# Attention feeding a feed-forward layer on one core: the order of two middle periods, and where one transpose, one copy and some stores stand

## The chip, the core and the metric

The kernel runs on one core of a Trainium2 chip. The metric is the device time of one execution in microseconds (us); the median of 3 runs of the kernel before is 207.83 us (207.78 to 207.98). The profiled execution has a span of 205.9 us, and its granted TensorE clock was 1.00 throughout. Engine names are those of the profile: PE multiplies matrices (PEld is its loading of weights), DVE is the vector engine, ACT the scalar engine, POOL issues the loads, SP issues stores and DMA transposes.

## What is computed

Attention with a local band of 96 keys and 8 global keys, over 4 batches, 8 heads, 768 rows and 64 elements per head. Its output, 3072 rows of 512, goes through a feed-forward layer with a squared ReLU.

```python
# q, k, v: (4, 8, 768, 64);  w_in: (512, 2048);  w_out: (2048, 512)
scores = q @ k.T / sqrt(64) + bias(head, distance)     # -1e9 outside band and globals
a = softmax(scores)
x = (a @ v) with heads side by side                    # (3072, 512)
h = x @ w_in
g = s * maximum(h, 0)**2 + b
out = g @ w_out                                        # (3072, 512), float32
```

## The kernel before

The rows are cut into 12 granules of 256 rows, three to a batch. Granules 0, 3, 6 and 9 are the first of their batch and need no older keys; the others do, through the copies `ko` and `vo`. A period j overlaps three granules: the attention of granule j, the first product (`P1`) of granule j-1 and the second product of granule j-2. For granules 0 to 2 the second product is plain (`P2`); from 3 on (`W0 = 3`) it is a Strassen-like scheme of seven products (`W_mm`) with sums made on DVE (`W_tw` of weights, `W_sw` of values). The order of instructions on every engine is the order of the calls in the program, and each engine works through its own list in order.

The helpers that matter, with the lines of the kernel before under which the profile files their instructions:

```python
def S_mm(j, hp):    # L414 PE: scores of one pair of heads into PSUM "scA" or "scB"
def S_post(j, hp):  # L427 ACT: exp;  then S_mul, L437/L441 DVE: times the template
def A(j, hp, tag):  # L470 PE: values times scores;  A_norm, L487+L488 DVE: divide
                    #   (tags "av": 1 buffer, "psh": 2 buffers, shared with P1)
def KO(j):          # L338+L341 DVE: keys of older blocks for granule j
def XB(j):          # L319, L327 SP: DMA transposes of keys and queries
def XT_dma(j):      # L531 SP: DMA transpose of x
def P1(j, fp, sq):  # L552 PE: 8 matmuls of 256 columns;  L568/L570 ACT: ReLU;
                    #   square: "act" on ACT at once (L576); "late" on DVE where Q()
                    #   is called (L589); else on DVE at the next PE group (L543)
def P2_mm(j, tb, part):   # L622 PE: 4 matmuls of 512 columns per part
def P2_raw(j, tb):        # L655 ACT: s * product, without the row vector bvec
def P2_bias(j, tb):       # L660 DVE: + bvec, and a store
def W_mm(j, n):           # L735 PE: 8 matmuls of 256 columns

def VO(j):                # values of older blocks
    ...
    nc.vector.tensor_copy(vo[:, :, :, 0:65], vaug[...])               # L363
    nc.vector.tensor_copy(vo[0:NG, :, :, 0:65], vaug[...broadcast])   # L366

def XT_pe(j, eng="act", tag="pso"):
    ... 8 x nc.tensor.transpose(...)        # L500 PE
    nc.scalar.copy(xT[j][:], ps[:])         # L506 ACT

def wsum_fin():
    ps = ps_h.tile([P, DM], F32, name="ps_b", tag="psh")
    ... 2 matmuls                                              # L613 PE
    nc.vector.tensor_scalar_mul(bvec[:], ps[:], b_bc[:])       # L614 DVE

def P2_out(j, tb):        # L640 DVE: s * product + bvec
    ...
    if tb == 1:
        P2_store_all(j)   # one store of 512 KB on SP
```

Periods 3 and 4 are built by `period`, which takes products from a list between the parts of the attention:

```python
def period(j, items, at, late=None, mid=()):
    SS(j, (0, 1))              # scores, exp, template of two pairs of heads
    run(items, at[0])
    A(j, 0)
    run(items, at[1])
    A(j, 1, "psh")
    run(list(mid), 100)
    SS(j, (2, 3))
    if j == 3:
        pace(pts[j, 2][0:1, 0, 0:1])
        load_granule(6)
    run(items, at[2])
    A(j, 2)
    if at[3]:
        KO(j + 1)
    run(items, at[3])
    A(j, 3, "psh")
    ...
    if late is None:
        XT_dma(j)
    if j + 1 < NJ:
        VO(j + 1)
    if j + 2 < NJ:
        XB(j + 2)
    if late is not None:       # period 3: wsum_fin, then x of granule 3
        run(items, 1)
        late()
        XT_pe(j, "act", "psh")
    run(items, 100)

P2b(0); P2b(1)                 # P2 of granule 1, second half, parts 0 and 1
for f in range(4):
    P1(2, f, "act" if f % 2 else "late")
Q(2, 0); Q(2, 2)
period(3, [P2b 2, P2b 3, P1(2, 4..7), P2(2, 0..3), P2_bias(0, 0), P2_bias(0, 1),
           P2_store_all(0)], (3, 1, 3, 1), wsum_fin, (W_tw 3 in two halves))

# [...] period 4: at = (4, 2, 3, 0), mid = (W_tw 2 second half, P2_bias(1, 1))
items = [(P1, 3, 0, "act"), (P2, 2, 4), (P1, 3, 1), (W_tw, 2, 0, 4)]
items += [(P2, 2, 5), (P2_bias, 1, 0)]
items += [(P1, 3, 2, "late"), (P1, 3, 3, "late"), (P2, 2, 6), (Q, 3, 2), (Q, 3, 3)]
items += [(P1, 3, 4, "act"), (P2, 2, 7), (P1, 3, 5, "act"), (P1, 3, 6),
          (W_tw, 4, 0, 4), (P1, 3, 7), (W_sw, 3, 3), (flush,), (W_tw, 4, 4, 8)]
```

From period 5 on `steady(j)` is used, which the change leaves as it is. It begins: scores of pairs 0 and 1, `W_mm(j-2, 1)`, `W_mm(j-2, 2)` (into "scA", so after the exp of the first scores), `P1` of j-1 twice, `A(j, 0)`, `P1`, `A(j, 1)`; on DVE the template products, `W_post` and `W_sw` stand between them.

Of the kernel before, what the change touches and what calls it, by code (L numbers as in the profile page):

```python
# [18 lines left out]
def kernel(  # L19
# [62 lines left out]
    def bg(j):  # L82
        return divmod(j, NGR)
# [33 lines left out]
    def load_granule(j):  # L117
        load_rows(j, "k")
        load_rows(j, "q")
        load_v(j)  # L120
# [3 lines left out]
    def pace(t):  # L124
        nc.gpsimd.tensor_copy(pdum[:], t)  # L125
# [183 lines left out]
    def XB(j, nms="kq"):  # L309
        if "k" in nms:  # L310
            XBk(j)
        if "q" in nms:
            XBq(j)
# [18 lines left out]
    def KO(j):  # L332
        b, g = bg(j)
        if g == 0:
            return
        ko = work.tile([P, HP, GB, P], BF16, name="ko", tag="ko", bufs=2)
        lo = (g * GB - 1) * P
        nc.vector.tensor_copy(  # L338
            ko[:].rearrange("p h a c -> p h (a c)"), kT[b % 2][:, :, lo : lo + GT]
        )  # L340
        nc.vector.tensor_copy(  # L341
            ko[:, :, :, 0:NG],
            kT[b % 2][:, :, 0:NG].unsqueeze(2).to_broadcast((P, HP, GB, NG)),
        )
        kos[j] = ko
# [9 lines left out]
            ko[:, :, :, 0:NG], kT[0][:, :, 0:NG].unsqueeze(2).to_broadcast((P, HP, GB, NG))  # L355
        )

    def VO(j):
        b, g = bg(j)
        if g == 0:  # L360
            return
        vo = work.tile([P, GB, H, VW], BF16, name="vo", tag="vo", bufs=2)
        nc.vector.tensor_copy(  # L363
            vo[:, :, :, 0:65], vaug[b % 2][:, g * GB - 1 : (g + 1) * GB - 1, :, 0:65]
        )
        nc.vector.tensor_copy(  # L366
            vo[0:NG, :, :, 0:65],
            vaug[b % 2][0:NG, 0:1, :, 0:65].to_broadcast((NG, GB, H, 65)),
        )
        vos[j] = vo  # L370

    sps = {}

# [69 lines left out]
    def SS(j, hps, which=None):  # L443
        for hp in hps:
            S_mm(j, hp, which=which)
        for hp in hps:
            S_post(j, hp)

    def A(j, hp, tag="av", norm=True, av=None):
        b, g = bg(j)  # L450
        first = g == 0
        pt = pts.pop((j, hp))
        if j not in xn:
            xn[j] = xpool.tile([P, GB, H, D], BF16, name="xn", tag="xn", bufs=2)
        if av is None:
            av = PS[tag].tile([P, GB, 2, 65], F32, name="ps_av", tag=tag)
        for i in range(GB):
            for hi in range(2):
                h = 2 * hp + hi
                if first:  # L460
                    ops = [(i, vaug[b % 2][:, i, h, 0:65])]
                    if i == 1:
                        ops.append((2, vaug[b % 2][:, 0, h, 0:65]))
                else:
                    ops = [
                        ((0, 2)[i], vaug[b % 2][:, g * GB + i, h, 0:65]),
                        ((1, 3)[i], vos[j][:, i, h, 0:65]),
                    ]
                for n_, (c, vv) in enumerate(ops):
                    nc.tensor.matmul(  # L470
                        av[:, i, hi, :],
                        lhsT=pt[:, hi, c * P : (c + 1) * P],
                        rhs=vv,
                        start=n_ == 0,
                        stop=n_ == len(ops) - 1,
                    )
        avs[j, hp] = av
        if norm:
            A_norm(j, hp)
            flush()  # L480
# [12 lines left out]
        )  # L493

    def XT_pe(j, eng="act", tag="pso"):
        xT[j] = xpool.tile([P, KC, GT], BF16, name="xT", tag="xT")
        ps = PS[tag].tile([P, KC, GT], BF16, name="ps_x", tag=tag)
        for hp in range(HP):
            for i in range(GB):
                nc.tensor.transpose(  # L500
                    ps[:, hp, i * P : (i + 1) * P],
                    xn[j][:, i, 2 * hp : 2 * hp + 2, :],
                    ident[:],
                )
        if eng == "act":
            nc.scalar.copy(xT[j][:], ps[:])  # L506
        else:
            nc.vector.tensor_copy(xT[j][:], ps[:])

    def XT_half(j, half, eng, tag):  # L510
        if half == 0:
# [16 lines left out]
    def XT_dma(j):  # L528
        xT[j] = xpool.tile([P, KC, GT], BF16, name="xT", tag="xT")
        for i in range(GB):  # L530
            nc.sync.dma_start_transpose(  # L531
                xT[j][:, :, i * P : (i + 1) * P],
                xn[j][:, i, :, :].rearrange("p h d -> p (h d)"),
            )
# [52 lines left out]
    def Q(j, fp):  # L587
        gs = late_sq.pop((j, fp))
        nc.vector.tensor_tensor(gs, gs, gs, ALU.mult)  # L589
# [18 lines left out]
        nc.vector.tensor_tensor(hl[:, 1, :], wsum[:, 0, :], hl[:, 0, :], ALU.subtract)  # L608

    def wsum_fin():  # L610
        ps = ps_h.tile([P, DM], F32, name="ps_b", tag="psh")
        for i in range(2):
            nc.tensor.matmul(ps[:], lhsT=ones_f[:], rhs=hl[:, i, :], start=i == 0, stop=i == 1)  # L613
        nc.vector.tensor_scalar_mul(bvec[:], ps[:], b_bc[:])  # L614
# [22 lines left out]
    def P2_out(j, tb):  # L637
        b, g = bg(j)
        o_sb = o_tile(j, tb)
        nc.vector.scalar_tensor_tensor(  # L640
            out=o_sb,
            in0=po[j, tb],
            scalar=s_bc[:],
            in1=bvec[:],
            op0=ALU.mult,
            op1=ALU.add,
        )
        if tb == 1:
            P2_store_all(j)

    raw = {}

    def P2_raw(j, tb):
        o_sb = o_tile(j, tb)
        nc.scalar.activation(o_sb, po[j, tb], ACT.Copy, scale=s_bc[:])  # L655
        raw[j, tb] = o_sb

    def P2_bias(j, tb, store=True):
        o_sb = raw[j, tb]
        nc.vector.tensor_tensor(o_sb, o_sb, bvec[:], ALU.add)  # L660
        if store:
            P2_store(j, tb)

    def P2_store_all(j):
        b, g = bg(j)
        t0 = b * S + g * GT
        nc.sync.dma_start(
            out[t0 : t0 + GT, :].rearrange("(i p) c -> p i c", p=P), o_t[j][:]
        )

    def P2_store(j, tb):
        b, g = bg(j)
# [101 lines left out]
    def W_rows(j):  # L774
        b, g = bg(j)
        t0 = b * S + g * GT
        return out[t0 : t0 + GT, :].rearrange("(p r) c -> p r c", r=2)

    def W_store(j):
        nc.sync.dma_start(W_rows(j), wt[j, "o"][:])  # L780

    def W(j, n, *sums):
        W_mm(j, n)
# [198 lines left out]
    def run(items, n):  # L982
        for _ in range(n):
            if items:
                f, *a = items.pop(0)
                f(*a)

    def P2b(c):
        if c == 0:
            po[1, 1] = ps_o.tile([P, DM], F32, name="ps_2", tag="pso")[:]  # L990
        P2_mm(1, 1, c)
        if c == 3:
            P2_raw(1, 1)

    def period(j, items, at, late=None, mid=()):
        SS(j, (0, 1))
        run(items, at[0])
        A(j, 0)
        run(items, at[1])
        A(j, 1, "psh")  # L1000
        run(list(mid), 100)
        SS(j, (2, 3))
        if j == 3:
            pace(pts[j, 2][0:1, 0, 0:1])
            load_granule(6)
        run(items, at[2])
        A(j, 2)
        if at[3]:
            KO(j + 1)
        run(items, at[3])  # L1010
        A(j, 3, "psh")
        if not at[3]:
            KO(j + 1)
        if late is None:
            XT_dma(j)
        if j + 1 < NJ:
            VO(j + 1)
        if j + 2 < NJ:
            XB(j + 2)
        if late is not None:  # L1020
            run(items, 1)
            late()
            XT_pe(j, "act", "psh")
        run(items, 100)

    P2b(0)
    P2b(1)
    for f in range(4):
        P1(2, f, "act" if f % 2 else "late")
    Q(2, 0)  # L1030
    Q(2, 2)
    period(
        3,
        [
            (P2b, 2),
            (P2b, 3),
            (P1, 2, 4),
            (P1, 2, 5, "act"),
            (P1, 2, 6, "act"),
            (P1, 2, 7, "act"),  # L1040
            (P2, 2, 0),
            (P2, 2, 1),
            (P2, 2, 2),
            (P2, 2, 3),
            (P2_bias, 0, 0, False),
            (P2_bias, 0, 1, False),
            (P2_store_all, 0),
        ],
        (3, 1, 3, 1),
        wsum_fin,  # L1050
        ((W_tw, 3, 0, 4), (W_tw, 3, 4, 8)),
    )

    def P1s(j, fp, n):
        P1(j, fp)
# [82 lines left out]
        r(7)  # L1138
        W_sw(m, 3)

    for j in range(4, NJ):
        m, l = j - 1, j - 2
        if l < W0:
            items = [(P1, m, 0, "act"), (P2, l, 4), (P1, m, 1), (W_tw, 2, 0, 4)]
            items += [(P2, l, 5), (P2_bias, 1, 0)]
            items += [(P1, m, 2, "late"), (P1, m, 3, "late"), (P2, l, 6), (Q, m, 2), (Q, m, 3)]
            items += [(P1, m, 4, "act"), (P2, l, 7), (P1, m, 5, "act"), (P1, m, 6), (W_tw, 4, 0, 4), (P1, m, 7), (W_sw, m, 3), (flush,), (W_tw, 4, 4, 8)]
            period(j, items, (4, 2, 3, 0), mid=((W_tw, 2, 4, 8), (P2_bias, 1, 1, False)))
        else:
            steady(j)  # L1150
    l, m = NJ - 2, NJ - 1
    r = lambda f: P1(m, f, "late")
    Q(l, 7)
# [72 lines left out]
```

The softmax here doesn't subtract the row's maximum and nothing guards it: scores larger than these inputs give would overflow.

## Time and profile before

| | busy us | share of the 205.9 us span |
|---|---|---|
| PE | 198.5 | 96% |
| PEld | 160.6 | 78% |
| DVE | 173.4 | 84% |
| ACT | 115.9 | 56% |
| POOL | 73.2 | 36% |

In the trace period 3 begins with the score matmuls at 50.92 us, period 4 at 62.42 us, and period 5, the first steady one, at 76.04 us. In those two periods DVE is busy 10.49 of 11.50 us and 12.98 of 13.62 us. Matmuls overlap in the pipeline: the time that one takes in a group's mean is longer than the step from its start to the start of the next one, so PE's pace is read from a run of equal matmuls, and a wait from a step that is longer than that.

### The profile page before, as it was taken

Reading aid. Unit: us, or ns where it says so; the run is one execution under the profiler, and the core shown is the slowest. Engines: PE = TensorE matmul, PEld = TensorE weight load, DVE = VectorE, ACT = ScalarE, POOL = GpSimd, SP = SyncE. Lnnn points to the kernel's source line nnn. Section 1 sums busy time; section 2 is a strip of 40 time slices with the busy share of each in tenths; the row PEclk is TensorE's granted clock in tenths of the full one; section 3 lists DMA queues with packets and bytes.
Section 4 is the critical chain, followed back from the end, with each engine's and each line's share of the span. In section 5 each row is a group of like instructions: output and inputs, shape, how many; then the busy total and the mean of one; then the engine's idle time right before and its main releaser. Section 6 shows DMA issues by size and latency. Waiting matters only on the chain.

```text
span 205.9 us, 5597 instructions
## 1 busy us (share of the span) xinstructions
PE 198.5 (96%) x2286; PEld 160.6 (78%) x2293; DVE 173.4 (84%) x415; ACT 115.9 (56%) x174; POOL 73.2 (36%) x98
## 2 busy tenths in 40 slices
PE   7988999999999999999999999999999999999993
PEld 2667776547766678988988988988988988988883
DVE  5897677699989989788799799788799799787693
ACT  5887588355878576536536536536446446424400
POOL 8993683848274019009009119019000000000000
PEclk9999999999999999999999999999999999999999
DMA  5999999999999969969999969999975140040022
GB/s 164 193 184 197 192 194 193 181 154 145 148 133 150 237 83 99 194 137 118 108 227 109 208 91 106 204 109 121 204 85 140 42 133 23 0 153 5 0 105 102
DMA packets 103962, 27.64 MB, mean 134 GB/s; under 512 B 91392, under 2 KB 102016, under 8 KB 103936
## 3 DMA queue, kind: packets, MB, share of 16 engines
q0 software_dynamic: 70976, 13.11, 83.5%
q1 hardware_dynamic: 31904, 13.64, 33.8%
q10 hardware_dynamic: 1056, 0.52, 0.9%
q8 instruction: 18, 0.29, 0.6%
q14 instruction: 8, 0.07, 0.2%
HBM read 27.26 MB, written 6.29 MB: 163 GB/s over the span
## 4 chain that ended last, share of the span: by engine, by line
PE 81%; DMA 5%; POOL 5%; DVE 4%; ACT 2%; issue 1%; SPq 0%; POOLq 0%; ACTq 0%
PE ps L552 37%; PE ps_w L735 15%; PE ps_wb L735 7%; PE ps L622 6%; PE ps_av L470 4%; PE ps_wa L735 4%; DMA w_in_bf<-in_moe_w_in_dram 4%; PE ps_s L414 4%; POOL vaug L112 2%; PE ps_2s L622 2%; DVE pt L441 2%; DMA xT<-xn 1%; DVE o_pr L660 1%; POOL w_in_bf L129 1%; ACT pt L427 1%
## 5 line engine op out<-in xcount | busy, mean ns | idle before, releaser
L552 PE MATMUL ps<-xT,w_in_bf 128*128 128x256 bf16 x768 | 96.5, 273 | 2.1 <-DMA w_in_bf<-in_moe_w_in_dram 1.2
L552 PEld LDWEIGHTS <-w_in_bf 128*128 128x128 bf16 x768 | 72.6, 98 | 13.0 <-DMA w_in_bf<-in_moe_w_in_dram 2.3
L570 ACT ACTIVATE gT<-ps 128x512 bf16<-128x512 f32 x72 | 43.1, 598 | 58.5 <-PE ps L552 56.4
L427 ACT ACTIVATE pt<-ps_s 128x1024 bf16<-128x1024 f32 (+1 forms) x48 | 43.0, 950 | 4.0 <-PE ps_s L414 4.0
L735 PEld LDWEIGHTS <-sw 128*128 128x128 bf16 x288 | 28.1, 98 | 3.4
L589 DVE TENSOR_TENSOR gT<-gT 128x512 bf16<-128x512 bf16 x73 | 27.6, 415 | 1.7 <-ACT gT L570 1.6
L112 POOL DMA_DIRECT2D vaug<-in_v_dram x24 | 21.6, 912 | 4.1 <-DMA w_out_bf<-in_moe_w_out_dram 1.7
L441 DVE TENSOR_TENSOR pt<-pt,tmpl 128x1024 bf16<-128x1024 bf16 x31 | 20.7, 686 | 2.1 <-ACT pt L427 2.1
L735 PEld LDWEIGHTS <-gT 128*128 128x128 bf16 x208 | 19.8, 98 | 3.2 <-issue 0.2
L488 DVE TENSOR_TENSOR xn<-ps_av,rc 128x256 bf16<-128x256 f32 x48 | 20.4, 424 | 1.7
L125 POOL COPY pdum<-xT 1x1 bf16<-1x1 bf16 x5 | 2.5, 509 | 50.5 <-DMA xT<-xn 50.5
L622 PE MATMUL ps<-w_out_bf,gT 128*128 128x512 bf16 x74 | 18.8, 379 | 0.4 <-issue 0.2
L735 PE MATMUL ps_w<-tw,sw 128*128 128x256 bf16 x144 | 18.7, 273 | 0.0
L745 DVE SCALAR_TENSOR_TENSOR u<-ps_w,s_bc,bvec 128x256 f32<-128x256 f32 x27 | 12.9, 479 | 6.4 <-PE ps_w L735 6.4
L470 PEld LDWEIGHTS <-pt 128*128 128x128 bf16 x352 | 15.4, 98 | 3.3 <-DVE pt L441 1.2
L568 ACT ACTIVATE gT<-ps 128x512 bf16<-128x512 f32 x23 | 13.6, 598 | 6.9 <-PE ps L552 6.7
L104 POOL DMA_DIRECT2D qnat<-in_q_dram x18 | 16.0, 904 | 2.8 <-DMA w_out_bf<-in_moe_w_out_dram 1.4
L104 POOL DMA_DIRECT2D knat<-in_k_dram x18 | 15.9, 892 | 1.8 <-issue 1.5
L470 PE MATMUL ps_av<-vaug,pt 128*128 128x65 bf16 x224 | 16.2, 193 | 0.2 <-DVE pt L441 0.2
L622 PEld LDWEIGHTS <-gT 128*128 128x128 bf16 x96 | 8.7, 97 | 8.1
L487 DVE RECIPROCAL rc<-ps_av 128x4 f32<-128x4 f32 x48 | 8.7, 181 | 6.6 <-PE ps_av L470 6.4
L414 PE MATMUL ps_s<-qT,kT 64*128 64x128 bf16 x224 | 12.5, 218 | 0.1
(102 smaller groups left out, 242.4 us busy)
## 6 DMA issues: line engine op xcount, KB each, us to landing
out_dram<-o_pr SPq DMA_DIRECT2D x10, 512.0 KB, 6.0
vaug<-in_v_dram POOLq DMA_DIRECT2D x24, 128.0 KB, 8.0
knat<-in_k_dram POOLq DMA_DIRECT2D x22, 128.0 KB, 6.5
qnat<-in_q_dram POOLq DMA_DIRECT2D x22, 128.0 KB, 8.0
w_in_bf<-in_moe_w_in_dram POOLq DMA_DIRECT2D x8, 256.0 KB, 8.3
w_out_bf<-in_moe_w_out_dram POOLq DMA_DIRECT2D x4, 512.0 KB, 9.8
out_dram<-o_pr SPq DMA_DIRECT2D x3, 256.0 KB, 2.5
raw<-in_q_dram ACTq DMA_DIRECT2D x2, 256.0 KB, 4.9
```

Source lines behind the costliest of these rows:

```text
L104: nc.gpsimd.dma_start(t[:, i, :, :], src[b, :, sb * P : (sb + 1) * P, :].rearrange("h p d -> p h d"))
L112: nc.gpsimd.dma_start(vaug[b % 2][:, sb, :, 0:D], v[b, :, sb * P : (sb + 1) * P, :].rearrange("h p d -> p h d"),)
L414: nc.tensor.matmul(ps[:, hi, oc * P : (oc + 1) * P], lhsT=kt[r, :], rhs=qT[j][r, hp, i * P : (i + 1) * P], start=not biased, stop=not bias ...
L427: nc.scalar.activation(pt[:, :, 0:n], ps[:, :, 0:n], ACT.Exp, scale=QSCALE)
L441: nc.vector.tensor_tensor(x, x, m.unsqueeze(2).to_broadcast((P, 2, GB, 2 * P)), ALU.mult)
L470: nc.tensor.matmul(av[:, i, hi, :], lhsT=pt[:, hi, c * P : (c + 1) * P], rhs=vv, start=n_ == 0, stop=n_ == len(ops) - 1,)
L488: nc.vector.tensor_tensor(xn[j][:, :, 2 * hp : 2 * hp + 2, :], av[:, :, :, 0:D], rc[:].to_broadcast((P, GB, 2, D)), ALU.mult,)
L552: nc.tensor.matmul(ps[:, i, :], lhsT=w_in_bf[:, kc, fc * P : (fc + 1) * P], rhs=xT[j][:, kc, :], start=(kc == 0), stop=(kc == KC - 1),)
L570: nc.scalar.activation(gs.rearrange("p f (r t) -> p f r t", r=2), ps[:].rearrange("p f (t r) -> p f r t", r=2), ACT.Relu,)
L589: nc.vector.tensor_tensor(gs, gs, gs, ALU.mult)
L622: nc.tensor.matmul(po[j, tb], lhsT=gT[j][:, fc, tb * P : (tb + 1) * P], rhs=w_out_bf[:, fc, :], start=(fc == 0), stop=(fc == FC - 1),)
L735: nc.tensor.matmul(wt[j, ps], lhsT=lhs[:, f, :], rhs=rhs[:, f, :], start=first and f == 0, stop=f == HF - 1, skip_group_check=True,)
```

## The change

It writes periods 3 and 4 out as a fixed order of calls in place of `period`. Its aims are to let the data that PE asks for be ready when PE comes to it, and to have less work of DVE between the scores and the products that use them.

- The scores of period 3 come one product later against the list: after three parts of P2 of granule 1, two P1 groups and the fourth part.
- `wsum_fin` moves from the end of period 3 to its start, and takes PSUM buffer "av".
- x of granule 3 is still transposed on PE, now between the fourth part of P2(2, first half) and the scores of period 4; its copy on ACT is called after those scores.
- The two copies of `VO(4)` are called apart, with P2 parts between them.
- In period 4 the P2 parts of granule 2 come first and the P1 groups of granule 3 later; three squares of P1(3), which were on ACT, are on DVE.
- The additions of `bvec` to granules 0 and 1 are spread over both periods.
- `P2_out` stores each 128 rows by themselves; `W_store` of granules 3 to 8 stores its two interleaved rows apart.

```diff
-    def VO(j):
+    def VO(j, part=None):
 [...]  # part 0: the first copy, part 1: the second, None: both
     def XT_pe(j, eng="act", tag="pso"):
+        XT_mm(j, tag)          # the eight transposes
+        XT_cp(j, eng)          # the copy to SBUF
 [...]
     def wsum_fin():
-        ps = ps_h.tile([P, DM], F32, name="ps_b", tag="psh")
+        ps = ps_av.tile([P, DM], F32, name="ps_b", tag="av")
 [...]  # P2_out
-        if tb == 1:
-            P2_store_all(j)
+        t0 = b * S + g * GT + tb * P
+        nc.sync.dma_start(out[t0 : t0 + P, :], o_sb)
 [...]  # W_store
-        nc.sync.dma_start(W_rows(j), wt[j, "o"][:])
+        if j < W0 + 6:
+            for r in range(2):
+                nc.sync.dma_start(W_rows(j)[:, r, :], wt[j, "o"][:, r, :])
+        else:
+            nc.sync.dma_start(W_rows(j), wt[j, "o"][:])
 [...]  # in place of period() for 3 and 4:
+    for c in range(3):
+        P2b(c)
+    P1(2, 0, "late")
+    P1(2, 1, "act")
+    P2_mm(1, 1, 3)
+    SS(3, (0, 1))
+    P1(2, 2, "late")
+    P2_raw(1, 1)
+    wsum_fin()
+    P1(2, 3, "act")
+    Q(2, 0)
+    P2_bias(0, 0)
+    P1(2, 4)
+    A(3, 0)
+    P1(2, 5, "act")
+    A(3, 1, "psh")
+    Q(2, 2)
+    W_tw(3, 0, 4)
+    [S_mm, S_post, S_mul of pairs 2 and 3]
+    W_tw(3, 4, 8)
+    pace(pts[3, 2][0:1, 0, 0:1])
+    load_granule(6)
+    P1(2, 6, "act")
+    P1(2, 7, "act")
+    P2(2, 0)
+    A(3, 2)
+    A(3, 3, "psh")
+    KO(4)
+    P2(2, 1)
+    VO(4, 0)
+    P2(2, 2)
+    P2(2, 3)
+    VO(4, 1)
+    XB(5)
+
+    XT_mm(3, "psh")
+    SS(4, (0, 1))
+    XT_cp(3, "act")
+    P2(2, 4)
+    P2(2, 5)
+    P2_bias(0, 1)
+    W_tw(2, 0, 4)
+    A(4, 0)
+    P2(2, 6)
+    A(4, 1, "psh")
+    [S_mm, S_post of pairs 2 and 3]
+    S_mul(4, 2)
+    P2_mm(2, 1, 3)
+    P1(3, 0, "late")
+    P2_bias(1, 0)
+    S_mul(4, 3)
+    W_tw(2, 4, 8)
+    A(4, 2)
+    P1(3, 1, "late")
+    A(4, 3, "scB")
+    XT_dma(4)
+    P2_out(2, 1)
+    Q(3, 0)
+    KO(5)
+    P1(3, 2, "late")
+    VO(5)
+    XB(6)
+    Q(3, 1)
+    P2_bias(1, 1, False)
+    P1(3, 3)
+    Q(3, 2)
+    P1(3, 4)
+    P1(3, 5)
+    W_tw(4, 0, 4)
+    P1(3, 6)
+    P1(3, 7)
+    flush()
+    W_sw(3, 3)
+    W_tw(4, 4, 8)
```

More of the change, by code (lines that the diff above doesn't have):

```diff
@@ L361, in VO @@
             return
[L362 to L370, printed above, removed]
+        if part != 1:
+            vos[j] = work.tile([P, GB, H, VW], BF16, name="vo", tag="vo", bufs=2)
+        vo = vos[j]
+        if part != 1:
+            nc.vector.tensor_copy(
+                vo[:, :, :, 0:65],
+                vaug[b % 2][:, g * GB - 1 : (g + 1) * GB - 1, :, 0:65],
+            )
+        if part != 0:
+            nc.vector.tensor_copy(
+                vo[0:NG, :, :, 0:65],
+                vaug[b % 2][0:NG, 0:1, :, 0:65].to_broadcast((NG, GB, H, 65)),
+            )
     sps = {}
@@ L495, in XT_pe, with XT_mm @@
     def XT_pe(j, eng="act", tag="pso"):
+        XT_mm(j, tag)
+        XT_cp(j, eng)
+    xps = {}
+    def XT_mm(j, tag):
         xT[j] = xpool.tile([P, KC, GT], BF16, name="xT", tag="xT")
@@ L504, in XT_pe, with XT_cp @@
                 )
+        xps[j] = ps
+    def XT_cp(j, eng):
         if eng == "act":
-            nc.scalar.copy(xT[j][:], ps[:])
+            nc.scalar.copy(xT[j][:], xps[j][:])
         else:
-            nc.vector.tensor_copy(xT[j][:], ps[:])
+            nc.vector.tensor_copy(xT[j][:], xps[j][:])
     def XT_half(j, half, eng, tag):
@@ L662, in P2_bias @@
             P2_store(j, tb)
[L664 to L669, printed above, removed]
     def P2_store(j, tb):
@@ L993, in P2b @@
             P2_raw(1, 1)
[L995 to L1029, printed above, removed]
-    Q(2, 0)
-    Q(2, 2)
[L1032 to L1052, printed above, removed]
+    for c in range(3):
+        P2b(c)
@@ new lines @@
+    P1(2, 0, "late")
[6 more added lines that the diff above has]
+    P1(2, 3, "act")
+    Q(2, 0)
+    P2_bias(0, 0)
[3 more added lines that the diff above has]
+    A(3, 1, "psh")
+    Q(2, 2)
+    W_tw(3, 0, 4)
+    for hp in (2, 3):
+        S_mm(3, hp)
+    for hp in (2, 3):
+        S_post(3, hp, mul=False)
+    S_mul(3, 2)
+    S_mul(3, 3)
+    W_tw(3, 4, 8)
+    pace(pts[3, 2][0:1, 0, 0:1])
+    load_granule(6)
@@ new lines @@
+    P1(2, 6, "act")
[20 more added lines that the diff above has]
+    A(4, 1, "psh")
+    for hp in (2, 3):
+        S_mm(4, hp)
+    for hp in (2, 3):
+        S_post(4, hp, mul=False)
+    S_mul(4, 2)
+    P2_mm(2, 1, 3)
+    P1(3, 0, "late")
@@ L1139, in steady @@
         W_sw(m, 3)
[L1141 to L1150, printed above, removed]
+    for j in range(5, NJ):
+        steady(j)
     l, m = NJ - 2, NJ - 1
```

## The prediction

> **What bounds the kernel now.** I read the page first (busy shares), then the busy time by stage, then the waits of the stage that changes, then the chain of work, and last the timeline around each wait.
>
> Page and stages. Columns of the second fence: stretch, its length, then busy us (instructions) of PE, PEld, DVE, ACT, POOL, the clock, the DMA engines' share and GB/s.
>
> ```profile
> PE 198.5 (96%) x2286; PEld 160.6 (78%) x2293; DVE 173.4 (84%) x415; ACT 115.9 (56%) x174; POOL 73.2 (36%) x98
> ```
> ```profile
> 50.92:62.42 11.50, 11.23 (x113) 7.57 (x116) 10.49 (x25) 9.44 (x16) 6.39 (x9) 1.00 1.92 140
> 62.42:76.04 13.62, 13.15 (x143) 9.46 (x144) 12.98 (x29) 9.67 (x15) 1.41 (x2) 1.00 1.41 162
> 76.04:90.00 13.96, 13.89 (x171) 12.28 (x171) 12.13 (x29) 8.53 (x13) 5.52 (x7) 1.00 1.40 144
> ```
>
> PE sets the pace of the whole. The change touches only 46 to 78 us, and there DVE is nearly full: 95% in period 4. So two limits lie close together. The chain of work in period 4 shows what that means (start, us, what):
>
> ```profile
> 62.49 0.57 PE ps_s L414 x16
> 63.06 0.03 issue
> 63.09 0.75 DVE o_pr L640
> 63.84 1.20 DVE o_pr L660 x2
> 65.04 1.20 DVE pt L441 x2
> 66.25 0.60 DVE tw L691
> ...
> 70.08 1.22 DVE pt L441 x2
> 71.30 0.05 issue
> 71.34 0.42 PE ps_av L470 x8
> ```
>
> The chain leaves PE at the scores (L414), runs over DVE for eight microseconds, and returns to PE at A (L470). In it three output instructions (L640, L660) stand in front of the template products (L441) that A waits for. The waits that follow, and the pace:
>
> ```profile
> 68.93 0.77 PEld L552 LDWEIGHTS <-w_in_bf 128*128 128x128 bf16 x8 [0.46 <-DVE xn L488]
> 71.34 0.20 PE L470 MATMUL ps_av<-vaug,pt 128*128 128x65 bf16 x1 [0.18 <-DVE pt L441]
> 73.33 2.78 PE L552 MATMUL ps<-xT,w_in_bf 128*128 128x256 bf16 x24
> 77.72 1.03 PE L735 MATMUL ps_wa<-w_out_bf,gT 128*128 128x256 bf16 x8
> ```
>
> The third line gives PE's step: 24 matmuls in 2.78 us, of which the last takes its full 273 ns, so (2.78 - 0.27) / 23 = 109 ns each and 0.87 us for a P1 group or a W product. In the same way a P2 part takes 0.86, a set of scores 0.45 (0.34 in period 3), A 0.23 (0.17), x's transposes 0.45, the bvec product 0.43.
>
> **The ceiling of a gain.** From the scores at 50.92 to P1(4, 0) at 78.58 are 27.7 us. Work: 12 P1 groups 10.5, 10 P2 parts 8.6, two W 1.7, five sets of scores 2.0, eight A 1.6, bvec and x 0.9: 25.4. Between other work and scores PE's step is 0.1 longer each way in nearly every case, whatever is waited for: 10 x 0.1 = 1.0. What is left, 1.3 us, are waits: 0.35 at each of the first two lines above (PE's starts go from 68.49 to 68.94, where the step is 0.11, and from 70.97 to 71.34, where it is 0.03), 0.2 to 0.25 before the second W product (its buffer is freed by the exp that ends at 77.66), the rest in pieces of 0.04 to 0.2. So no order of this work can be worth more than 1.3 us, 0.6%. The steady periods hold next to no waits, and the waits before 46 us aren't touched.
>
> **What the Trainium skill says.** "Perfetto Trace Analysis", Identifying the Most-Contended Engine, warns that PE's busy share is no measure of how full it is; this trace agrees, since the 0.35 us gap at 68.5 shows as 0.18 or less of idle time, the pipeline's tail covering the rest. The same page, Optimization Strategy, says that the most contended engine can change from stage to stage; here DVE is at 95% in period 4 and at 87% in 76 to 90. "VectorE: DVE Perf Modes", The perf-mode tier table, holds two-input operations on bf16 to half the speed of the best copies; the trace agrees (template product of 1024 in 0.69 us, copy of 1040 in 0.43), so squares moved to DVE aren't cheap. "DMA: Bandwidth & Descriptors", Issuing engines are not separate DMA queues, lets all issued transfers share the same engines; whether the earlier stores slow transposes no run here shows yet.
>
> **Part by part.** Counts on PE are equal before and after: nothing is removed or added there. On ACT three squares (L576, 0.63 each) go; on DVE three come, at a step of 0.34 (two adjacent squares at 73.72 and 74.05), so DVE gains 1.0 us of work, against 1.8 us of idle time that it had from 50.92 to 78.58 (27.66 less 25.87 busy; 0.46 of it at 75.7, 0.39 at 58.5, the rest small). All else on DVE is moved. I laid the new order out by hand, with the steps above for PE, and on DVE 0.6 for a template product, a bias addition, a W_tw or a W_sw, 0.66 for P2_out, 0.56 for a norm, 0.55 for KO, 0.82 for VO; on ACT 0.9 to 1.0 for an exp, 0.6 for a ReLU. Scores of period 3 fall at 50.9 as before. Then, at each point where PE may wait (us from the span's start):
>
> | PE comes to | at | what it needs is ready at |
> |---|---|---|
> | A(3, 1) | 55.4 | 55.6: buffer "psh", after a ReLU on ACT |
> | A(3, 2), A(3, 3) | 58.9, 59.1 | 58.4, 59.1 (template) |
> | x's transposes | 61.9 | 60.8 (norm) |
> | P2(2, 4) | 63.0 | 62.8 (P2_out frees its buffer) |
> | A(4, 0), A(4, 1) | 64.8, 65.9 | 64.6, 65.5 (template) |
> | A(4, 2), A(4, 3) | 68.5, 69.7 | 68.5, 69.7 (template) |
> | scores of period 5 | 75.4 | 73.0 (KO) |
> | second W product | 76.9 | 77.1 (exp frees the buffer) |
> | A(5, 0), A(5, 1) | 79.8, 80.9 | 79.1, 80.8 (template) |
>
> Before, scores of period 5 stood at 76.04 and A(5, 1) at 81.45: PE would be 0.5 to 0.6 us earlier. The waits at 68.5 and 71.0 go (-0.7), a wait at A(3, 1) comes (+0.2). DVE however ends its template product of A(5, 1) at 80.8, later than the 80.34 of before. Its lead over PE, 1.1 us there before, falls to 0.1. In the steady period that follows the next DVE idle (0.73 before L745 at 84.30) takes most of this up, but the product for A(5, 3), which before ended at 85.98 with A some 0.1 behind, comes about 0.2 late. I subtract 0.5, and take back 0.1 to 0.2 for meetings that are ties: net -0.4, 207.4 us.
>
> The transposes of keys and queries of granule 5 now stand on SP behind the store of P2_out(2, 0), so they start at some 63 and not at 55.80 and 59.75. With 3.3, 2.6 and the step between them they end near 69.5, before KO(5) at 72.4. Split stores: 512 KB in 6.0 us becomes twice 256 KB, 2.5 us each; nothing on PE waits for a store. I give both nothing. VO in two parts: the copies took 0.75 and 0.83 in period 3 against 0.43 and 0.43 in period 4, while POOL issued loads; those loads are still issued then, so I expect no less time, but P2_out is let in between.
>
> **Rivals.** (1) DVE becomes the bound: the 1.0 us of squares is not hidden and appears as waits at W products and A of period 5. For it: 95% busy, a lead of 0.1 at A(5, 1). Against it: 1.8 us of idle time, and the steady periods have gaps. It makes +0.3 to +1.0: 208.1 to 208.8. (2) The full ceiling: the ties fall well, ACT has less to do and frees "psh" sooner: -0.9 to -1.2, 206.6 to 206.9. For it: ACT loses 1.9 us of work in period 4. Against it: the second W product still needs its exp. (3) Transposes of granule 5 are late, through the store ahead of them and loads of granule 6 beside them: KO(5) waits on DVE and all behind it. Slack is about 3 us, so it needs a doubling; it would make 209 to 211.
>
> **Range and chances.** The ceiling gives the low side, 206.8; rival 1 gives the high side, 208.4. Rival 3 alone reaches 2%, which is 4.2 us. Chances: faster by over 2% 0.01, within 2% 0.97, slower by over 2% 0.02.
>
> **What would show it.** Right: period 5's scores near 75.4, no wait at P1 of granule 3 or A(4, 3) above 0.15, DVE's idle time in this stretch down by about 1 us, A(5, 1) near 80.9. Wrong: a wait above 0.3 at A(4, 2), A(5, 1) or A(5, 3) for L445 (the template in the new file), KO(5) waiting for a DMA, or scores of period 4 off 62.4 by over 0.3.

## The result, and the profile after

The changed kernel takes 206.98 us (median of 4 runs, 206.67 to 207.06), the kernel before 207.81 us (207.56 to 207.98) beside it: ratio 0.9958, 95% interval 0.9941 to 0.9975. That is 0.8 us less; 0.4 was predicted, in a range of 206.8 to 208.4.

Busy time of the page after:

```profile
PE 198.1 (97%) x2293; PEld 160.5 (78%) x2293; DVE 173.8 (85%) x418; ACT 114.2 (56%) x171; POOL 76.4 (37%) x98
```

ACT has three instructions fewer and DVE three more: the squares. The stages, cut at the same events as before (first scores of periods 3, 4 and 5, and 14 us of period 5):

```profile
50.49:61.99 11.50, 11.50 (x123) 8.38 (x122) 10.77 (x26) 9.42 (x16) 6.06 (x9) 1.00 2.31 149
61.99:74.85 12.86, 12.86 (x146) 9.47 (x145) 12.05 (x29) 8.96 (x12) 1.75 (x3) 1.00 1.76 192
74.85:88.80 13.95, 13.88 (x170) 12.18 (x170) 13.14 (x32) 8.44 (x12) 8.99 (x7) 1.00 1.33 120
```

Period 3 is as long as before, to the hundredth: 11.50. Period 4 is 0.76 us shorter, 12.86 against 13.62, and PE is busy in all of it by this count (waits of 0.02 to 0.08 us are left in its steps). DVE is less full there (94% against 95%) and fuller in period 5 (94% against 87%): work was pushed from one to the other. The chain of work in period 4, whose eight microseconds on DVE were shown before, now never leaves PE:

```profile
61.62 0.45 PE ps_x L510 x8
62.07 0.55 PE ps_s L418 x16
62.62 1.83 PE ps L635 x8
64.45 0.24 PE ps_av L474 x8
64.70 0.86 PE ps L635 x4
65.56 0.24 PE ps_av L474 x8
...
69.68 5.25 PE ps L565 x48
74.93 0.02 issue
74.96 0.35 ACT gT L583
...
75.45 1.03 ACT pt L431
76.48 0.04 issue
76.52 1.03 PE ps_wa L741 x8
```

(L418 scores, L635 P2, L474 A, L565 P1, L741 W.) The one turn off PE that is left goes through ACT at 75: the exp of period 5's first scores frees the buffer of the second W product. DVE around the scores of period 4:

```profile
61.66 0.75 DVE L653 SCALAR_TENSOR_TENSOR o_pr<-ps,s_bc,bvec 128x512 f32<-128x512 f32 x1 [0.27 <-PE ps L635]
62.33 0.79 DVE L371 COPY vo<-vaug 8x1040 bf16<-8x1040 bf16 x1
63.49 0.69 DVE L445 TENSOR_TENSOR pt<-pt,tmpl 128x1024 bf16<-128x1024 bf16 x1 [0.38 <-ACT pt L431]
64.41 0.69 DVE L445 TENSOR_TENSOR pt<-pt,tmpl 128x1024 bf16<-128x1024 bf16 x1 [0.22 <-ACT pt L431]
```

The template products (L445) now wait for the exp on ACT, so DVE is ahead of it; before, two bias additions stood between the output and them, and DVE was behind.

**Where the 0.8 us comes from.** I cut both traces by single events: the last weight load that both orders have in common, that of P2 of granule 1, second half, part 1 (46.91 us before and 46.49 after), the last weight load of the first scores of period 3 (51.16 and 50.73), the third weight load of A(5, 1) (81.48 and 80.30), the end. The piece from the first scores of period 3 to A(5, 1) is called the stage below. It is 30.31 us before and 29.57 after, -0.74. Ahead of it the pieces differ by 0.42 and 0.02; behind it 124.41 became 124.47, +0.06. From the first event to the end that is -0.70, against -0.83 in the medians; what makes up the difference is not shown. The 0.42 is not the change's: the order up to the first event is the same, and it came at 46.4 to 47.1 us over all traces, with the new order at both ends of that range.

### The profile page after: what moved, and what is told of

The parts are those of the page before. It is cut to its first block, busy times and chain, and to the rows that moved or that the text cites. A ratio compares the mean times of both kernels' runs of the same rounds, so it can differ in the third digit from the quotient of the medians.

```text
span 204.8 us, 5622 instructions
## 1 busy us (share of the span) xinstructions
PE 198.1 (97%) x2293; PEld 160.5 (78%) x2293; DVE 173.8 (85%) x418; ACT 114.2 (56%) x171; POOL 76.4 (37%) x98
## 4 chain that ended last, share of the span: by engine, by line
PE 89%; POOL 4%; DMA 3%; ACT 1%; issue 0%; DVE 0%; POOLq 0%; ACTq 0%
PE ps L565 41%; PE ps_w L741 15%; PE ps L635 9%; PE ps_wb L741 7%; PE ps_av L474 5%; PE ps_s L418 4%; PE ps_wa L741 4%; DMA w_in_bf<-in_moe_w_in_dram 3%; POOL vaug L112 2%; PE ps_2s L635 2%; ACT gT L583 1%; POOL knat L92 1%; POOL qnat L92 1%; ACT pt L431 1%; PE ps_e L828 0%; PE ps_x L510 0%
## 5 line engine op out<-in xcount | busy, mean ns | idle before, releaser
L565 PE MATMUL ps<-xT,w_in_bf 128*128 128x256 bf16 x768 | 96.2, 273 | 1.6 <-DMA w_in_bf<-in_moe_w_in_dram 1.5
L565 PEld LDWEIGHTS <-w_in_bf 128*128 128x128 bf16 x768 | 72.7, 98 | 11.7 <-DMA w_in_bf<-in_moe_w_in_dram 1.8
L741 PEld LDWEIGHTS <-sw 128*128 128x128 bf16 x288 | 28.1, 98 | 3.4
L602 DVE TENSOR_TENSOR gT<-gT 128x512 bf16<-128x512 bf16 x74 | 28.1, 415 | 1.7 <-ACT gT L583 1.6
L125 POOL COPY pdum<-xT 1x1 bf16<-1x1 bf16 x5 | 6.0, 1206 | 46.6 <-DMA xT<-xn 46.6
L445 DVE TENSOR_TENSOR pt<-pt,tmpl 128x1024 bf16<-128x1024 bf16 x31 | 20.8, 686 | 2.7 <-ACT pt L431 2.7
L741 PEld LDWEIGHTS <-gT 128*128 128x128 bf16 x208 | 19.7, 98 | 3.2 <-issue 0.2
L635 PE MATMUL ps<-w_out_bf,gT 128*128 128x512 bf16 x80 | 19.2, 379 | 0.0
L741 PE MATMUL ps_w<-tw,sw 128*128 128x256 bf16 x144 | 18.7, 273 | 0.0
L474 PEld LDWEIGHTS <-pt 128*128 128x128 bf16 x352 | 15.2, 98 | 3.0 <-DVE pt L445 0.8
L474 PE MATMUL ps_av<-vaug,pt 128*128 128x65 bf16 x224 | 16.0, 193 | 0.0
L635 PEld LDWEIGHTS <-gT 128*128 128x128 bf16 x96 | 8.8, 98 | 8.9
L418 PE MATMUL ps_s<-qT,kT 64*128 64x128 bf16 x224 | 12.5, 218 | 0.1
```

The lines of the kernel that those rows point to most:

```text
L418: nc.tensor.matmul(ps[:, hi, oc * P : (oc + 1) * P], lhsT=kt[r, :], rhs=qT[j][r, hp, i * P : (i + 1) * P], start=not biased, stop=not bias ...
L445: nc.vector.tensor_tensor(x, x, m.unsqueeze(2).to_broadcast((P, 2, GB, 2 * P)), ALU.mult)
L474: nc.tensor.matmul(av[:, i, hi, :], lhsT=pt[:, hi, c * P : (c + 1) * P], rhs=vv, start=n_ == 0, stop=n_ == len(ops) - 1,)
L565: nc.tensor.matmul(ps[:, i, :], lhsT=w_in_bf[:, kc, fc * P : (fc + 1) * P], rhs=xT[j][:, kc, :], start=(kc == 0), stop=(kc == KC - 1),)
L635: nc.tensor.matmul(po[j, tb], lhsT=gT[j][:, fc, tb * P : (tb + 1) * P], rhs=w_out_bf[:, fc, :], start=(fc == 0), stop=(fc == FC - 1),)
L741: nc.tensor.matmul(wt[j, ps], lhsT=lhs[:, f, :], rhs=rhs[:, f, :], start=first and f == 0, stop=f == HF - 1, skip_group_check=True,)
```

## The experiments

Two theories. **Q** (mine): PE's order costs nothing by itself; the gain is waits of PE for DVE in period 4, removed by taking instructions out of DVE's list between an output and the template products. **P**: the order of products in period 4 is what counts (P2 first, P1 of granule 3 late). Smaller rivals are named with the runs. All twelve ran where the kernel before took 209.1 to 209.2 us, so the ratios are to runs of it on the same chip, and their intervals are wide against the effects. The stage is the better measure: e1 (the old order) repeats the 30.31 of before as 30.34, e12 (the changed kernel again) 29.57 as 29.58.

| run | stage, us | ratio to before, 95% interval |
|---|---|---|
| before; changed | 30.31; 29.57 | changed 0.9958 (0.9941 to 0.9975) |
| e1 stores only | 30.34 | 1.0012 (0.9997 to 1.0028) |
| e2 new period 3, old 4 | 30.22 | 1.0004 (0.9983 to 1.0026) |
| e3 old period 3, new 4 | see text | 1.0023 (1.0001 to 1.0045) |
| e4 bias additions first | 30.13 | 0.9973 (0.9948 to 0.9998) |
| e5 three squares on ACT | 29.81 | 0.9979 (0.9965 to 0.9994) |
| e6 VO whole | 29.87 | 0.9963 (0.9947 to 0.9979) |
| e7 P1 ahead of second W | 29.58 | 0.9972 (0.9937 to 1.0006) |
| e8 e7 and three squares | 29.58 | 0.9960 (0.9940 to 0.9979) |
| e9 e7 and two squares | 29.33 | 0.9943 (0.9916 to 0.9970) |
| e10 e9, scores later | 28.63 + 0.87 | 0.9936 (0.9905 to 0.9966) |
| e11 e2, x transposed earlier | 29.62 | 0.9956 (0.9931 to 0.9982) |
| e12 changed, again | 29.58 | 0.9935 (0.9914 to 0.9957) |

### e1: the stores alone

```diff
 # the kernel before, with
-        if tb == 1: P2_store_all(j)
+        nc.sync.dma_start(out[t0 : t0 + P, :], o_sb)        # per 128 rows
 # and W_store split in two for granules 3 to 8
```

> The kernel before with nothing but the split stores. Theory Q (the gain is waits of PE on DVE in period 4, taken away by what stands in DVE's list between scores and products): no change, 0.0 us within 0.2, and 30.5 us from the first scores of period 3 to A(5, 1), as before. Rival S (stores that no longer hold up the queue give part of it): 0.2 to 0.4 us faster, and the stage shorter than 30.3. Rival H (the gain lies before 46 us, in when the weights arrive, and is chance): P1(0, 3) and what follows may start anywhere from 0.4 us earlier to as before, in this kernel too.

Stage 30.34, and 124.45 behind it: nothing, as Q has it. Rival S falls. The first event is at 46.84, as before (46.91), so nothing speaks for H as a gain of the change; that part just varies (46.36 to 47.09 over all traces).

### e4: two bias additions in front of the template products

```diff
     XT_mm(3, "psh")
+    P2_bias(0, 1)
+    P2_bias(1, 0)
     SS(4, (0, 1))
 # and both taken out where they stood, after the products
```

> The changed kernel with two bias additions moved on DVE, from after the template products of period 4 to before them; PE's order and all work are the same. Theory Q: the first template product ends 1.0 to 1.2 us later, A(4, 0) waits 0.7 to 0.9 us, and the gain of the change is lost: 0.5 to 0.9 us slower than the changed kernel. Rival P: within 0.2 us of the changed kernel.

Its DVE and weight loads:

```profile
64.12 0.79 DVE L371 COPY vo<-vaug 8x1040 bf16<-8x1040 bf16 x1
64.83 1.27 DVE L673 TENSOR_TENSOR o_pr<-o_pr,bvec 128x512 f32<-128x512 f32 x2
66.03 1.27 DVE L445 TENSOR_TENSOR pt<-pt,tmpl 128x1024 bf16<-128x1024 bf16 x2
```
```profile
64.34 1.41 PEld L635 LDWEIGHTS <-gT 128*128 128x128 bf16 x8
66.76 0.30 PEld L474 LDWEIGHTS <-pt 128*128 128x128 bf16 x8 [1.00 <-DVE pt L445]
```

The additions (L673) take 1.2 us ahead of the products, and A (L474) waits for them; PE's step before A is 0.67 us too long. The stage is 0.56 longer, with the same order on PE. Q holds, P falls for this piece. It is 0.56 and not 0.67, since the small waits that the changed kernel has later, at A(4, 2) and A(4, 3), 0.02 and 0.08, are gone.

### e3 and e2: one period new, the other old

```diff
 # e3: periods as
-    [new period 3]
+    [period(3, ...) of the kernel before, stores split]
     [new period 4, without XT_mm, XT_cp and P2_bias(0, 1), which period 3 has done]
```

> Period 3 in the old order (bvec, two bias additions and the output still ahead of the scores' products on DVE), period 4 in the new one. Theory Q: P2(2, 4) waits some 0.8 us for its buffer and A(4, 0) up to 1 us for its template product, so the time is as before or up to 0.7 us above it. Rival P: nearly the whole gain, 0.6 to 0.8 us faster than before.

The granted clock was 0.50 to 0.75 from 54 to 58 us, ahead of the second scores of period 3, and 1.00 from there on, so I count from those to A(5, 1): 26.10 us, against 25.93 before and 24.65 in the changed kernel. As before or above: Q holds, P falls. The chain:

```profile
66.13 0.57 PE ps_s L418 x16
66.70 0.03 issue
66.73 0.76 DVE o_pr L653
67.50 0.04 issue
67.54 1.89 PE ps L635 x8
```

P2 (L635) waits for the output (L653) that frees its buffer: 0.93 us, where 0.8 was expected. In the old period 3 bvec and the copies keep that output back. New order on PE, old list on DVE: no gain.

```diff
 # e2: [new period 3], then
+    XT_pe(3, "act", "psh")
+    P2_bias(0, 1)
+    [period(4, ...) of the kernel before, its items unchanged]
```

> Period 3 in the new order, period 4 in the old one (x of granule 3 transposed and one bias addition ahead of the scores of period 4). Theory Q: DVE has one output and the two copies' second half in front of the template products instead of bvec, one output and two additions, so part of the waits goes: 0.2 to 0.5 us faster than before, 0.3 to 0.6 slower than the changed kernel; a wait stays at A(4, 3). Rival P (what counts is that in period 4 the second products come first and P1 of granule 3 late): no gain here, 0.0 within 0.15.

Stage 30.22: a gain of 0.1 only, which would speak for P. The waits show why not:

```profile
PE ps L565 <- ACT xT L519: 0.5, 1, 0.5
```

P1(3, 0) follows the scores at once in the old order, and x of granule 3, now transposed right ahead of the scores, isn't copied yet. PE's step is 0.62 us too long there. My edit had added a wait of its own, so the run tells nothing on Q and P. Hence e11.

### e11: the same with x transposed one product earlier

```diff
     P2(2, 2)
+    XT_pe(3, "act", "psh")      # as in the kernel before, ahead of P2(2, 3)
     P2(2, 3)
```

> New period 3 and old period 4 as in the earlier run, but with granule 3's x transposed ahead of P2(2, 3), as in the kernel before, so that P1(3, 0) doesn't wait for its copy. Theory Q: what remains are the waits that the bias additions and the output make on DVE in period 4: a wait of 0.2 to 0.4 us at A(4, 3) and little at P1: stage 29.7 to 29.9 us, between 29.57 (changed) and 30.31 (before). Rival P (the order of products in period 4 is what counts): 30.2 or more.

29.62: within 0.05 of the changed kernel, with the old period 4, its early P1 groups and its squares on ACT. A wait of 0.17 at A(4, 3) is left (0.2 to 0.4 was expected, so even less is lost). So the new period 3 is enough: bvec and one addition are off DVE before the scores of period 4. The new period 4 brings 0.05. This run does not separate PE's order in period 3 from DVE's list; e4 does that, with PE's order unchanged. And Q's first half is too strong: e2 shows that an order on PE can bring a wait of its own, there for ACT. P falls for the order as a whole; what the new order of period 4 needs instead is care, as e3, e4 and e6 show, because only 1.7 us of products stand between its scores and A(4, 0), and 2.6 in the old.

### e6: the two copies of VO(4) together

```diff
-    VO(4, 0)
+    VO(4)
 [...]
-    VO(4, 1)
```

> The changed kernel with both copies of VO(4) together, ahead of the output P2_out(2, 0) on DVE. Theory Q: the output ends 0.7 us later, at some 63.1, P2(2, 4) wants its buffer at 62.5, so PE waits 0.5 to 0.7 us there, of which A(4, 0) gives back what it would have waited anyway (none now): 0.4 to 0.7 us slower than the changed kernel. Rival: the exp that waited for the output in the trace of the changed kernel goes ahead as before and only 0.1 us is lost.

```profile
62.97 0.81 DVE L371 COPY vo<-vaug 8x1040 bf16<-8x1040 bf16 x1
63.71 0.73 DVE L653 SCALAR_TENSOR_TENSOR o_pr<-ps,s_bc,bvec 128x512 f32<-128x512 f32 x1
```
```profile
64.49 1.89 PE L635 MATMUL ps<-w_out_bf,gT 128*128 128x512 bf16 x8 [0.32 <-DVE o_pr L653]
```

The output stands behind the second copy, P2 waits for its buffer, 0.39 us in steps; the stage is 0.30 longer (0.4 to 0.7 expected, 0.1 by the rival: nearer to Q). The exp, of which the rival spoke, started 0.44 us after its scores did, as in the changed kernel: it was not what the output held up. The cut in two is worth its 0.3, but only by what it lets pass: the copies take 0.74 and 0.79 apart, 0.73 and 0.81 together.

### e5, e7, e8, e9: what is left around period 5

```diff
 # e5: for f in 0, 1, 2 (e9: 0, 1)
-    P1(3, f, "late")  and  Q(3, f)
+    P1(3, f, "act")
 # e7: in steady(5), as in later periods
     W_mm(l, 1)
+    r(0)                        # P1(4, 0)
     W_mm(l, 2)
-    r(0)
 # e8: e7 and e5;  e9: e7 and two squares
```

> The changed kernel with the squares of P1(3, 0), (3, 1) and (3, 2) on ACT at once, where ACT is idle, and off DVE. Theory Q: PE stays where it is, because the scores of period 5 and the second W product don't wait for DVE; DVE's lead at A(5, 1) rises from 0.1 to about 1 us; time 0.0 to 0.1 us less than the changed kernel. Rival D (the squares moved to DVE cost the change part of its gain): 0.3 us less or more.

29.81, 0.24 slower than the changed kernel: neither theory had that. In the groups of P1(3, 2) to (3, 7), changed kernel (first fence) and e5:

```profile
69.52 5.40 PE L565 MATMUL ps<-xT,w_in_bf 128*128 128x256 bf16 x48
```
```profile
71.23 5.65 PE L565 MATMUL ps<-xT,w_in_bf 128*128 128x256 bf16 x48
```

In e5 the same 48 matmuls take 0.25 more: the step from the 24th to the 25th, before P1(3, 5), is 0.36 and not 0.11. The third square sits on ACT between the ReLUs of P1(3, 2) and P1(3, 3); the second of these ends at 74.07, and P1(3, 5), which takes its buffer, starts at 74.09. (The expectation of e9 below puts this wait at P1(3, 4); counted in groups of eight matmuls it is at P1(3, 5).) Squares on DVE cost the change nothing.

> The changed kernel with P1(4, 0) in front of the second W product in period 5, as in the later steady periods, so that the exp which frees the W product's buffer has 0.9 us more. Theory: the wait of 0.23 us at the second W product goes, but A(5, 1) then waits for its template product, which ends with only 0.07 us to spare: 0.0 to 0.1 us faster than the changed kernel. Rival: DVE isn't that close, and the whole 0.2 us is gained.

As the theory has it: stage 29.58. The wait of 0.23 at the second W product is gone, and comes back at A(5, 1):

```profile
81.27 0.30 PEld L474 LDWEIGHTS <-pt 128*128 128x128 bf16 x8 [0.35 <-DVE pt L445]
```

> Both: P1(4, 0) ahead of the second W product, and three squares of P1(3) on ACT. Theory: with 1 us more lead of DVE the 0.23 us is kept: 0.2 us faster than the changed kernel, some 206.7 to 206.8. Rival: x of granule 4 lands too late for the earlier P1(4, 0), or DVE isn't what held A(5, 1): no gain, or as much as without the squares.

No gain, 29.58, though not for a reason that was named: the wait at A(5, 1) is gone (4.85 us from period 5's scores to it, against 5.10), and the 0.25 at P1(3, 5) of e5 stands in its place.

> P1(4, 0) ahead of the second W product, and only two squares, of P1(3, 0) and (3, 1), on ACT, where the run with three had ACT late by 0.25 us for the buffer of P1(3, 4). Theory: DVE's lead at A(5, 1) rises by 0.67 us, so the wait there (0.24 with no square moved) goes and none comes at P1(3, 4): from the first scores of period 3 to A(5, 1) 29.3 to 29.4 us, against 29.57 in the changed kernel. Rival: ACT is late again: 29.55 or more.

29.33, as expected: 0.24 less than the changed kernel, with both waits gone. A (L474) now follows P1 with no wait:

```profile
82.56 0.78 PEld L565 LDWEIGHTS <-w_in_bf 128*128 128x128 bf16 x8
83.35 0.39 PEld L474 LDWEIGHTS <-pt 128*128 128x128 bf16 x8
```

The times don't resolve this: median 208.16 us against 208.14 for e12 beside it. What probably hides it is the next point.

### e10 and e12: the first scores of period 3

```diff
 # e10: e9, and
-    SS(3, (0, 1))
     P1(2, 2, "late")
     P2_raw(1, 1)
+    SS(3, (0, 1))
 [...]
     P1(2, 4)
-    A(3, 0)
     P1(2, 5, "act")
+    A(3, 0)
```

> The same, and the first scores of period 3 one P1 group later still, with A(3, 0) after P1(2, 5). In the traces of these experiments PE waits 0.5 to 1.2 us at those scores for the DMA transpose of granule 3's queries; in those of the kernel before and of the changed kernel it lands just in time. Theory: with 0.9 us more the wait is 0 to 0.3 where it was 0.5 to 1.2, and if the transpose is in time anyway nothing is gained or lost within 0.15; from there to A(5, 1) the stage is 0.87 us shorter, as one P1 group lies ahead of it. Rival: the template products come late to A(3, 1) and PE loses 0.3 us or more there.

> The changed kernel once more, beside the others on one chip. From the first scores of period 3 to A(5, 1) 29.57 us within 0.03; what lies ahead of it may differ by up to 1.2 us with the landing of granule 3's queries.

Every experiment, e1 with the old order among them, has a wait at those scores that the first two traces lack. In e12:

```profile
PE ps_s L418 <- DMA qT<-qnat: 1.7, 1, 1.7
```

It is 0.3 to 2.8 us of idle time in the twelve profiles: the second of the two DMA transposes of granule 3's queries lands late, at 51.5 to 53.9 us, against 50.6 and 50.3 in the first two traces. The transpose itself is hardly slower (7.1 to 8.0 us from issue to landing, 9.0 in e9, against 7.4 and 7.1). It is issued later, at 44.1 to 45.1 against 43.2, within 0.2 us after the landing of the load that feeds it; and that load, issued at 33.8 to 34.2 in all traces, took 10.1 to 11.1 us against 9.1 and 9.0. So the load is what came late; why it was slower is not shown. In e12 the wait ends at 52.4, 1.9 us later than in the first trace of the same kernel, where up to 1.2 was expected. In e10 the wait is 1.0 with the scores 0.9 later, against 1.7 in e12; the two can't be compared, as the landing moves too. As an estimate from e10's trace: the queries landed at 52.51, so scores at the earlier place would have waited some 0.9 longer. My 0 to 0.3 was wrong. The stage with the P1 group that now lies ahead of it is 29.50, 0.17 worse than e9, by a wait of 0.22 at P1(2, 7). The median of e10 is lower than those beside it, 207.66 us against 208.14 (e12) and 209.11 (before), but the intervals overlap widely: that it beats the changed kernel is not shown. By the stage, e9 is the best version.

## Why the prediction was right, and where it was off

Right in direction and range; half of the size. The mechanism that it named, waits of PE behind DVE's list in period 4, is the one that the experiments show.

- **Two limits close together, DVE in front of A in period 4.** Shown by e4 and e3, and by e11 from the other side. The ceiling of 1.3 us stands: 0.74 taken by the change, 0.98 by e9.
- **"The waits at 68.5 and 71.0 go (-0.7)".** They went: steps too long by 0.34 before P1(3, 3) and by 0.35 before A(4, 3) became 0 and 0.08.
- **"A wait at A(3, 1) comes (+0.2)".** It came, 0.09.
- **The net of -0.5 to -0.6 at A(5, 1).** It is -0.74. The term that was mis-sized is the small waits of the old order that I had put into "the rest in pieces" and then not credited: 0.13 before P1(2, 6), 0.06 at P1(3, 0), 0.04 and 0.06 at A(4, 0) and A(4, 2), 0.29 together. In the new trace 0.05, 0, 0 and 0.02 are left of them. With the two points above this is the whole: 0.34 + 0.27 + 0.22 - 0.09 = 0.74.
- **"I take back 0.1 to 0.2 for meetings that are ties".** The ties cost nothing: 124.41 us behind A(5, 1) before, 124.47 after. The product for A(5, 3), which I had 0.2 late, ended at 84.89 and A began at 84.95 without a wait. DVE's lead there is 0.06 where it was 0.11, so its next idle time took up nearly the whole delay.
- **DVE's lead at A(5, 1) falls to 0.1.** It ends at 80.20, PE comes at 80.25. e7 shows how real that is.
- **DVE's idle time down by about 1 us.** Wrong: 1.8 us before, 26.90 - 25.36 = 1.5 after (50.49 to 77.39, where P1(4, 0) starts). The work that was counted on came later: DVE's busy time in the first 14 us of period 5 rose by 1.0, from 12.13 to 13.14.
- **Transposes of granule 5 behind a store, stores split, VO in two parts.** No effect of the first: KO(5) started at 71.81 with no wait. But the times that I gave were those for which SP is busy issuing, not those of the transfers: the keys landed at 70.0 and 70.6 us, 7.1 and 6.4 after their issue, and the queries at 71.1 and 71.5. The part that KO(5) reads had 1.8 us to spare, and not some 3. None of the second (e1). For the third I had "no less time, but P2_out is let in between"; e6 gives that 0.3 us.
- **Scores one product later** I gave nothing, and in the trace they come 4.24 us after the first event against 4.26: not later at all, because as much work was moved ahead of them as was taken away. So the change doesn't help where their queries are late.
- **Signs.** One of those named for being wrong came: the scores of period 4 at 62.0, off 62.4 by 0.4. It says nothing against the mechanism, as the whole trace stood 0.4 earlier already at 46 us and period 3 took 11.50 us in both. By the same shift period 5's scores at 74.85 (75.4 predicted) and A(5, 1) at 80.25 (80.9) come to 75.3 and 80.7.

Rival 1 (squares make DVE the bound) falls by e5, rival 2 was nearer in size than my own number, rival 3 didn't occur.

## What to carry to other kernels

When PE and a vector engine are both nearly full, look at what stands in the vector engine's list between the event that PE has just finished and the instruction that PE will need next; move what has no deadline (here a row vector and additions to finished outputs) to the other side of it. Judge such edits by the time between two events in the trace, which repeated within 0.03 us here, when the total varies by more than the effect. A wait taken away may only have covered the next one: e7 gained nothing until two squares were moved as well, and the third square moved cost it all again.

## What was not expected of the hardware

- In a run of two-input instructions on DVE, each starts 0.08 us before the one ahead is recorded as ended: products of 0.68 us come every 0.60 us.
- A copy of 1040 elements on 8 partitions took 0.79 us at 62 us, while POOL was issuing loads, and 0.43 us at 72.8, while it was not; the one on 128 partitions 0.74 and 0.43. That the issuing is the cause wasn't tried.
- PE pays 0.095 us in nearly every change between scores (64 rows) and other matmuls, in each direction, in all traces, also where nothing is waited for.
- A DMA transpose of queries or keys took 7 to 10 us from issue to landing at 41 to 54 us, of which SP was busy for 1.2 to 2.7. A load that took 10.1 to 11.1 us and not 9.1 delayed one of them, and PE then sat idle for 0.3 to 2.8 us, where the change gains 0.8.
